# Pooled attention before two gated layers: the attention's order of work regrouped into six cycles of three key chunks

## The chip, the cores and the metric

The kernel runs on one core of a Trainium2 chip. The metric is the device time of one execution in microseconds. The kernel before was timed twice, 773.44 and 771.93 us, median 772.68 us. A further execution was profiled; its own time was 777.65 us and its span, from the first to the last instruction, 775.9 us.

## What is computed

Inputs are q, k and v of shape (2, 8, 1152, 64): two batches of eight heads. Attention pools q by two (576 query rows against 1152 keys), then two gated layers follow. Cut to what matters:

```python
q_pool = q.reshape(B, H, S // 2, 2, D).mean(axis=3)
scores = scale * np.matmul(q_pool, k.transpose(0, 1, 3, 2))
scores = scores - np.max(scores, axis=-1, keepdims=True)
attn = np.exp(scores); attn = attn / (np.sum(attn, axis=-1, keepdims=True) + 1e-09)
x = np.matmul(attn, v)           # -> (B * 576, 512)
xn = x / rms(x) * rms_g          # 1152 tokens, d_model 512, d_ff 1536
x = (silu(xn @ w_gate) * (xn @ w_val)) @ w_out
out = (sigmoid(x @ w_gate2) * (x @ w_val2)) @ w_out2
```

All is float32. Products that need the precision are made of three float32r products of split halves (high x high, high x low, low x high); turns and the products with v are plain float32. Weights arrive as 64-bit words and are turned into float32 and split on the core.

## The kernel before, in words

**Pairs.** The 16 heads are handled as 8 pairs; the two heads of a pair use the two 64-row lanes of TensorE at once (`LANES`). The 576 query rows of a head are chunks of 128, numbered 1 to 4, and 64 rows that are left; those of both heads together are chunk 0.

**Scores.** `s_unit` (L435 on) makes the scores of one query chunk against 384 keys: six products (L454) into two of the three `s` banks, for chunk 0 three products (L451) into one. For each bank `top` (L459, VectorE) writes the negated scores into an `e` tile and keeps the running minimum; from the second 384 keys on it starts from the minimum before, read as a pointer operand. After the third, `expo` (L463, ScalarE) takes the exponential of the 1152 columns in place, with row sums. A pair has 15 units, 27 tops, 9 exponentials; there are 10 `e` tiles.

**Turns and products with v.** `t_unit` (L480 on) turns 128 keys of the exponentials into a tile `t` of two PSUM banks (two such tiles exist), one bank a lane. `PARTS` gives two parts of a pair: chunks 1, 2 and 0 (ten turns a key chunk, L291, one copy of 640 columns), then 3 and 4 (eight turns, L498, two key chunks in one tile, one copy of 1024). The copy into `et` is ScalarE's (L510) or, where `E_DVE` says so, VectorE's (L508). `av_unit` (L526) multiplies v with the copies into the one `o` bank, in groups of two to five key chunks, right behind the copies (`AV_SLOTS`). `o_step` then turns the result back (L552), copies it (L563) and normalises it on GpSimd (L561).

**Order.** Every step is put by hand into an agenda: `at(g, rank, fn)`. Slots g run in order, ranks within a slot, then the order of registration; each engine executes its own instructions in the order in which the agenda emits them. A pair has 18 slots, one for each key chunk and part. The scores of the next pair lie in the slots of this one by a list:

```python
S_SLOTS = (-12, -9, -5, -8, -7, -6, -4, -3, -2, 0, 1, 2, 3, 4, 5)
AV_SLOTS = ({2: 3, 5: 6, 8: 9}, {3: 4, 8: 9})
E_DVE = ((2, 5, 8), (3, 7))
```

**Other work in the attention.** `prep_pair` turns k and q of the next pair (L291 into kT and qT, also in the two `t` tiles), ScalarE copies them (L350) and GpSimd splits them (L129, L130). `pool_q` (L325) sums q on GpSimd. `load_pair`, `load_v` and `w_load` issue on SP's queue. Five chunks of weights are converted during the attention (L197 to L240). `x_steps` does the rms norm: for the first batch during the last pairs, for the second at the end (L582 to L624, turns L603). From `END` on come the two layers (L683 to L822); their first four groups of products are interleaved with the last norm steps (`UP_SLOTS`).

Of the kernel before, what the change touches and what calls it, by code (L numbers as in the profile page):

```python
# [16 lines left out]
P = 128  # L17
# [5 lines left out]
S_SLOTS_FIRST = (-8, -7, -6, -5, -4, -3, -2, -1, 0, 1, 2, 3, 4, 5, 6)  # L23
S_SLOTS = (-12, -9, -5, -8, -7, -6, -4, -3, -2, 0, 1, 2, 3, 4, 5)
UNITS_FIRST = [(c, u) for u in range(3) for c in (3, 4)] + [(c, u) for c in (0, 1, 2) for u in range(3)]
UNITS = [(c, u) for c in range(5) for u in range(3)]
AV_SLOTS = ({2: 3, 5: 6, 8: 9}, {3: 4, 8: 9})
E_DVE = ((2, 5, 8), (3, 7))

PREP = ((1, 2, 3), (-5, -3, -1))  # L30
POOL_Q, LOAD, LOAD_V = -8, 0, 1
FIRST_K, FIRST_Q = (-7, -5), -4

W_SLOTS, W_SPLIT = (11, 12, 13, 14, 15), 8
W_WORDS, W_EARLY = 5, 4

X_SQUARES = ((-39, -37, -40), (-27, -30))
X_ROOTS = (-20, -17)
X_NORMS = ((-10, -15, -16), (-13, -11))
X_TURNS = ((-7, -12, -13), (-9, -8))  # L40
X_LAST = ((-3, -2, -2), (5, 6))

UP_SLOTS = (0, 2, 4, 7)
UP_GATES = (2, 4, 7, 9)
UP_SPLITS = (3, 5, 8, 10)
# [3 lines left out]
def tile_attention_moe_moe(ctx, tc, q, k, v, w_gate1, w_val1, w_out1, rms_g, w_gate2, w_val2, w_out2, out):  # L49
# [18 lines left out]
    NCA = 3  # L68
    PARTS = ((1, 2, 0), (3, 4))
# [29 lines left out]
    def two_banks(name):  # L99
        return ps.tile([P, 1024], F32, tag="t", bufs=2, name=name)  # L100
# [7 lines left out]
    osb = [ae.tile([P, 3 * P], F32, name="osb0"), ae.tile([P, 2 * P], F32, name="osb1")]  # L108
    nc.gpsimd.memset(osb[0][:, 5 * QH:6 * QH], 0.0)
# [172 lines left out]
    ready = {}  # L282
# [3 lines left out]
    def lanes(t, n, blocks):  # L286

        for x, (rows, cols) in enumerate(blocks):
            for j, r in enumerate(LANES):
                if rows[j] is not None:  # L290
                    nc.tensor.transpose(t[:, 512 - (1 - j) * 64 * n + x * 64:512 - (1 - j) * 64 * n + x * 64 + 64], rows[j][r, cols], ident[r, r])  # L291
        return t[:, 512 - 64 * n:512 + 64 * n]

    def turned(t):
        return t.rearrange("p (h c f) -> p h c f", h=2, f=QH)
# [4 lines left out]
    def load_pair(p):  # L300
        b, hp = divmod(p, NPAIR)
        kr = ap.tile([P, NK, P], F32, tag="kraw", bufs=1, name="kraw")
        qr = ap.tile([P, 2, NQC, 2 * D], F32, tag="qraw", bufs=1, name="qraw")
# [29 lines left out]
    def k_group(p, c0, c1, kr):  # L333
        t = lanes(two_banks("kT"), c1 - c0, [((kr[:, c], kr[:, c]), slice(0, P)) for c in range(c0, c1)])
        return t, kq[p][0][:, c0 * P:c1 * P], kq[p][1][:, c0 * P:c1 * P], 1.0

    def q_group(p, cs, qs):
        t = lanes(two_banks("qT"), len(cs), [((qs[:, c], qs[:, c]), slice(0, P)) for c in cs])
# [20 lines left out]
    def prep_pair(g0, p):  # L359
        alloc_pair(p)  # L360
        kr, qs = raw[p]
        slots = [g0 + x for x in PREP[p > 1]]
        at(slots[0], 3, lambda: prep_step(slots[0], k_group(p, 0, 5, kr)))
        at(slots[1], 3, lambda: prep_step(slots[1], q_group(p, (1, 2, 3, 4, 0), qs)))
        at(slots[1] + 1, 22, lambda: diagonal(p))
        at(slots[2], 3, lambda: prep_step(slots[2], k_group(p, 5, NK, kr)))

    def prep_first():


        def room():
            return ap.tile([P, NSU * SU], F32, tag="e", bufs=10, name="first")
# [4 lines left out]
        def load_q(j, c0, c1):  # L377
            qs = q[0, j].rearrange("(s two) d -> s (two d)", two=2)
            if c0 == 0:
                for r, x in ((slice(0, QH), SQ - QH), (slice(QH, P), 0)):  # L380
                    nc.sync.dma_start(qr[j][r, 0, :], qs[x:x + QH, :])
                c0 = 1
            nc.sync.dma_start(qr[j][:, c0:c1, :], qs[(c0 - 1) * P:(c1 - 1) * P, :].rearrange("(c p) e -> p c e", p=P))

        def load_k(j, c0, c1):
            nc.sync.dma_start(kr[:, c0:c1, j * D:(j + 1) * D], k[0, j].rearrange("(p c) d -> p c d", c=NK)[:, c0:c1])

        for j in range(2):
# [17 lines left out]
        def step(g, group, second):  # L406
# [6 lines left out]
            r = temp(t.shape[1])  # L413
# [18 lines left out]

        at(FIRST_Q, 1, rest)

    def s_unit(g, p, c, u):  # L435
# [20 lines left out]
        def top(j):  # L456

            m = emin[p, c, j]
            nc.vector.tensor_scalar(etile[p, c, j][:, kc], s[j], -1.0, m[:, u - 1:u] if u else None, op0=ALU.mult, op1=ALU.min, accum_out=m[:, u:u + 1])  # L459

        def expo(j):
            e = etile[p, c, j]
            nc.scalar.activation(e, e, AF.Exp, bias=emin[p, c, j][:, NSU - 1:NSU], scale=-1.0, accum_out=both_sums[p][:, j, c:c + 1])  # L463
# [5 lines left out]
        for j in heads:  # L469
            at(g, 17, lambda j=j: top(j))  # L470
        if u == NSU - 1:
            for j in heads:
                at(g + 1, 14, lambda j=j: expo(j))
            if c == 0:
                at(g + 2, 24, swap)
            ready.setdefault(p, []).append(c)
            if len(ready[p]) == NQC:
                at(g + 3, 25, lambda: nc.gpsimd.tensor_scalar(both_sums[p], both_sums[p], 1e-9, 1.0, op0=ALU.add, op1=ALU.mult))

    def t_unit(g, base, p, part, kc):  # L480

        ks = slice(kc * P, (kc + 1) * P)
        cs = PARTS[part]
        tiles = [(etile[p, c, 0], etile[p, c, 0]) for c in cs if c]
        tiles += [(etile[p, 0, 0], etile[p, 0, 0])] if 0 in cs else []
        tiles += [(etile[p, c, 1], etile[p, c, 1]) for c in cs if c]
        if part:

            odd = kc % 2
            n = 2 if odd or kc < NK - 1 else 1  # L490
            if not odd:
                tpair[p] = two_banks("eT"), []
            t, blocks = tpair[p]
            w = n * len(tiles) * 64
            for x, (a, b) in enumerate(tiles):
                for j, (y, r) in enumerate(((a, HP), (b, LP))):
                    o = 512 - (1 - j) * w + (odd * len(tiles) + x) * 64
                    nc.tensor.transpose(t[:, o:o + 64], y[r, ks], ident[r, r])  # L498
            if not odd and n == 2:
                return  # L500
            chunks = (kc - 1, kc) if odd else (kc,)
            t = t[:, 512 - w:512 + w]
        else:
            t = lanes(two_banks("eT"), len(tiles), [(x, ks) for x in tiles])
            chunks = (kc,)
        et = ae.tile([P, 1024], F32, tag="et", bufs=6, name="et")[:, 0:t.shape[1]]
        if kc in E_DVE[part]:
            at(g, 18, lambda: nc.vector.tensor_copy(woven(et), turned(t)))  # L508
        else:
            at(g, 12, lambda: nc.scalar.activation(woven(et), turned(t), AF.Copy))  # L510
        todo = ready.setdefault((p, part), [])
        n = et.shape[1] // len(chunks)
        todo += [(x, et[:, i * n:(i + 1) * n]) for i, x in enumerate(chunks)]
        if kc in AV_SLOTS[part]:
            now = list(todo)
            del todo[:]
            at(base + AV_SLOTS[part][kc], 4, lambda: av_unit(base + AV_SLOTS[part][kc], p, part, now))

    def av_unit(g, p, part, todo):
        if todo[0][0] == 0:  # L520
            acc_o[p, part] = bank("o", "o")
        o = acc_o[p, part]
        for kc, et in todo:
            n = et.shape[1] // 2
            for j, r in enumerate(LANES):
                nc.tensor.matmul(o[r, 0:n], vsb[p][:, j, kc], et[:, j * n:(j + 1) * n], start=(kc == 0), stop=(kc == NK - 1))  # L526
        if kc == NK - 1:
            at(g, 13, lambda: nc.scalar.activation(osb[part][:, 0:n], o[:, 0:n], AF.Copy))
# [339 lines left out]
```

## Time and profile before

| | |
|---|---|
| median of the two runs | 772.68 us |
| profiled execution, its own time | 777.65 us |
| its span | 775.9 us |
| TensorE busy (matmul / weight load) | 722.5 / 624.8 us |
| VectorE, ScalarE, GpSimd busy | 392.7, 382.9, 292.1 us |
| mean granted TensorE clock | 0.968 |
| attention's last product with v ends | 321.2 us |

In forty slices of the span TensorE is busy 7 to 9 tenths in the first 16, and 9 tenths or more in nearly all that follow; the granted clock is below full only in the first 17. A busy time in the profile overlaps with that of the next instruction, so what one instruction costs is read from the distance between two starts on the same engine, where neither waited. The clock's column is the share of full speed that was granted: 1.00 is the upper level, 2.4 GHz, and 0.50 the lower, 1.2 GHz.

### The profile page before, as it was taken

The page shows a single profiled execution, that of the slowest core. Times are in us where ns is not written, and L with a number is a line of the kernel's source. Part 1 is how long each engine was busy: PE and PEld are TensorE (multiplying, and loading weights), DVE is VectorE, ACT ScalarE, POOL GpSimd, SP SyncE. Part 2 cuts the span into 40 slices and gives each one's busy share as a digit, 9 for nine tenths or more (in the row PEclk, how much of TensorE's full clock was granted, in tenths as well). Part 3 has the DMA queues.
Part 4 walks back from the last instruction along what each step waited for, and adds up shares of the span by engine and source line. Part 5 has one row for each costly group of instructions (what it writes and reads, how often), then busy time and mean ns, then how long its engine had stood idle before and what let it go on. Part 6 is the DMA issues. An engine that isn't in the chain of part 4 may idle for free.

```text
span 775.9 us, 13594 instructions
## 1 busy us (share of the span) xinstructions
PE 722.5 (93%) x5420; PEld 624.8 (81%) x5420; DVE 392.7 (51%) x862; ACT 382.9 (49%) x684; POOL 292.1 (38%) x279
## 2 busy tenths in 40 slices
PE   7889797888888886999999999999999999999998
PEld 5666565555555563799999999999999999998886
DVE  5555565636464663468866675422345555454010
ACT  4665666656566654366544454432444454445000
POOL 3331514242424033046643455632434454347200
PEclk9999999979898997899999999999999999999999
DMA  8312314040401000033422232420312232223011
GB/s 193 103 42 56 86 39 104 21 106 19 105 18 59 2 2 1 10 99 117 128 82 82 82 109 82 129 90 28 109 55 81 83 108 62 76 82 109 0 55 68
DMA packets 66783, 55.92 MB, mean 72 GB/s; under 512 B 20896, under 2 KB 61856, under 8 KB 66720
## 3 DMA queue, kind: packets, MB, share of 16 engines
q1 hardware_dynamic: 66720, 55.06, 24.2%
q8 instruction: 42, 0.69, 0.4%
q14 instruction: 21, 0.17, 0.1%
HBM read 52.69 MB, written 2.36 MB: 71 GB/s over the span
## 4 chain that ended last, share of the span: by engine, by line
PE 82%; ACT 9%; issue 4%; DVE 4%; DMA 0%; POOL 0%; SPq 0%; ACTq 0%; DVEq 0%
PE acc L683 39%; PE o L526 10%; PE acc L793 10%; PE acc L822 9%; PE s L454 7%; ACT e L463 6%; ACT et L510 2%; PE eT L291 2%; PE eT L498 2%; PE s L451 1%; DVE e L459 1%; DVE et L508 1%; PE kT L291 1%; ACT kqt L350 1%; PE xT L603 0%
## 5 line engine op out<-in xcount | busy, mean ns | idle before, releaser
L683 PE MATMUL acc<-xh,w 128*128 128x384 f32 (+2 forms) x1184 | 295.3, 331 | 0.0
L683 PEld LDWEIGHTS acc<-xh,w 128*128 128x128 f32 x1184 | 211.8, 188 | 0.5 <-issue 0.4
L683 PE MATMUL acc<-xl,w 128*128 128x384 f32 (+2 forms) x592 | 195.6, 330 | 0.0
L240 POOL TENSOR_TENSOR w<-wr,w 128x512 fp32r<-128x512 f32 x68 | 99.9, 1469 | 166.9 <-ACT w L239 153.6
L459 DVE TENSOR_SCALAR_CACHE_REDUCE e<-s,m 128x384 f32<-128x384 f32 x144 | 83.8, 616 | 105.6 <-PE s L454 57.3
L683 PEld LDWEIGHTS acc<-xl,w 128*128 128x128 f32 x592 | 111.2, 188 | 0.0
L225 POOL TENSOR_TENSOR wr<-wsg,wr 128x512 uint32<-128x512 uint32 x72 | 93.6, 1300 | 45.5 <-DVE wsg L219 43.4
L454 PE MATMUL s<-kh,q 64*128 64x384 f32 x384 | 102.4, 409 | 8.5 <-DVE e L459 7.1
L526 PE MATMUL o<-et,vraw 128*64 128x256 f32 (+1 forms) x576 | 94.6, 474 | 0.7 <-DVE et L508 0.7
L463 ACT ACTIVATE e<-e,m 128x1152 f32<-128x1152 f32 x72 | 89.5, 1247 | 8.8 <-DVE e L459 8.8
L510 ACT ACTIVATE et<-eT 128x640 f32<-128x640 f32 (+2 forms) x72 | 54.7, 761 | 75.5 <-PE eT L498 43.6
L694 ACT ACTIVATE sg<-acc 128x384 f32<-128x384 f32 (+2 forms) x74 | 35.7, 482 | 102.4 <-PE acc L683 102.3
L454 PEld LDWEIGHTS s<-kh,q 64*128 64x128 f32 x384 | 56.0, 203 | 33.9 <-DVE e L459 21.4
L697 DVE TENSOR_TENSOR sg<-acc,sg 128x384 f32<-128x384 f32 (+2 forms) x74 | 40.4, 547 | 83.8 <-PE acc L683 78.6
L219 DVE SCALAR_TENSOR_TENSOR wsg<-wg,wsg 128x512 uint32<-128x512 uint32 x72 | 77.1, 1071 | 2.3
L793 PE MATMUL acc<-hh,w 128*128 128x384 f32 x288 | 73.2, 334 | 0.0
L197 ACT ACTIVATE wg<-wraw 128x512 f32<-128x512 f32 x72 | 48.3, 671 | 47.8 <-DVE wsg L219 42.5
L526 PEld LDWEIGHTS o<-et,vraw 128*64 128x64 f32 x576 | 42.9, 157 | 32.6 <-issue 10.7
L215 DVE TENSOR_SCALAR wsg<-wg 128x512 uint32<-128x512 uint32 x72 | 41.2, 572 | 35.0 <-POOL wr L225 34.9
L204 ACT ACTIVATE wr<-wraw 128x512 uint32<-128x512 uint32 x72 | 47.8, 665 | 9.5 <-POOL w L240 8.5
L793 PEld LDWEIGHTS acc<-hh,w 128*128 128x128 f32 x288 | 52.1, 188 | 0.0
L454 PE MATMUL s<-kl,q 64*128 64x384 f32 x192 | 50.9, 390 | 0.0
(104 smaller groups left out, 941.1 us busy)
## 6 DMA issues: line engine op xcount, KB each, us to landing
wraw<-in_moe_w_gate_dram SPq DMA_DIRECT2D x24, 512.0 KB, 3.6
wraw<-in_moe_w_val_dram SPq DMA_DIRECT2D x24, 512.0 KB, 3.6
wraw<-in_moe_w_out_dram SPq DMA_DIRECT2D x24, 512.0 KB, 3.5
vraw<-in_v_dram SPq DMA_DIRECT2D x16, 288.0 KB, 3.3
kraw<-in_k_dram SPq DMA_DIRECT2D x14, 288.0 KB, 4.9
qraw<-in_q_dram SPq DMA_DIRECT2D x14, 256.0 KB, 4.8
out_dram<-ob SPq DMA_DIRECT2D x9, 256.0 KB, 2.0
qraw<-in_q_dram SPq DMA_DIRECT2D x14, 64.0 KB, 4.5
```

The source lines that it names most:

```text
L197: nc.scalar.activation(g, wwords[n][:, :, 1].bitcast(F32), AF.Copy, scale=2.0 ** -112)
L219: nc.vector.scalar_tensor_tensor(x["s"], x["g"], 3, x["s"], op0=ALU.logical_shift_left, op1=ALU.bitwise_or)
L225: nc.gpsimd.tensor_tensor(x["r"], x["s"], x["r"], op=ALU.add)
L240: nc.gpsimd.tensor_tensor(t[:, 1], r, t[:, 0].bitcast(F32), op=ALU.subtract)
L454: nc.tensor.matmul(s[j], qt[r, x, QOF[c]:QOF[c] + P], ks[r, kc], start=(n == 0), stop=(n == 2))
L459: nc.vector.tensor_scalar(etile[p, c, j][:, kc], s[j], -1.0, m[:, u - 1:u] if u else None, op0=ALU.mult, op1=ALU.min, accum_out=m[:, u:u + 1])
L463: nc.scalar.activation(e, e, AF.Exp, bias=emin[p, c, j][:, NSU - 1:NSU], scale=-1.0, accum_out=both_sums[p][:, j, c:c + 1])
L510: at(g, 12, lambda: nc.scalar.activation(woven(et), turned(t), AF.Copy))
L526: nc.tensor.matmul(o[r, 0:n], vsb[p][:, j, kc], et[:, j * n:(j + 1) * n], start=(kc == 0), stop=(kc == NK - 1))
L683: nc.tensor.matmul(acc[:, 0:nt], wt[:, ws, dc * P:(dc + 1) * P], xs[:, dc], start=(dc == 0 and n == 0), stop=(dc == NDM - 1 and n == 2))
L793: nc.tensor.matmul(acc[t][:, 0:NTT], w[:, ws, (fc % 4) * P:(fc % 4 + 1) * P], hs[fc][:, cs], start=(fc == 0 and n == 0), stop=(fc == NFC - ...
L822: nc.tensor.matmul(acc[r][:, 0:DM], hs[fc][:, r * P:(r + 1) * P], w[:, ws, :], start=(fc == 0 and n == 0), stop=(fc == NFC - 1 and n == 2))
```

## The change

The agenda of the attention is made anew: a pair has six cycles of eight slots, a cycle turns three key chunks (cycles 0 to 2 for part 0, 3 to 5 for part 1). Chunk 0 moves to the second part, so `PARTS` is (1, 2) and (3, 4, 0). In a cycle the emitted order is: chunk 0's three units (cycle 1 only); turns of k, q or the result, if any; a first unit of scores; the turns of the first two key chunks into one `t` tile, half a bank each a lane; those of the third into the next `t` tile, with the three pieces of chunk 0 beside it in part 1; a second unit of scores; the products with v of the cycle before. Every key chunk is copied by itself: two by ScalarE, the third and chunk 0's pieces by VectorE. The running minimum becomes three separate maxima and a small reduction. There are 12 `e` tiles. q's load is issued behind `pool_q`, k's in cycle 1. The second batch's norm steps follow the last product directly. The core of the diff:

```diff
-S_SLOTS = (-12, -9, -5, -8, -7, -6, -4, -3, -2, 0, 1, 2, 3, 4, 5)
-AV_SLOTS = ({2: 3, 5: 6, 8: 9}, {3: 4, 8: 9})
-E_DVE = ((2, 5, 8), (3, 7))
-PREP = ((1, 2, 3), (-5, -3, -1))
+CYCLE, NCYC = 8, 6
+S_SUB, PREP_SUB, AV_SUB = (0, 4, 5), 0, 7
+S_UNITS = ((-5, 1, 1, 0), (-4, 0, 1, 1), (-4, 1, 1, 2), (-3, 0, 2, 0), (-3, 1, 2, 1), (-2, 0, 2, 2), (-2, 1, 3, 0),
+           (-1, 0, 3, 1), (-1, 1, 3, 2), (0, 0, 4, 0), (0, 1, 4, 1), (1, 0, 4, 2))
+C0_CYCLE = 1
+EXPS = {(1, 0): (-3, 1), (1, 1): (-3, 7), (2, 0): (-2, 7), (2, 1): (-1, 1), (3, 0): (0, 1), (3, 1): (0, 7),
+        (4, 0): (1, 7), (4, 1): (2, 1), (0, 0): (2, 7)}
+E_DVE = ((2,), (2,), (2,), (2, 3), (2, 3), (2, 3))
+PREP = ((0, 1, 2), (-3, -2, 0))
...
-    PARTS = ((1, 2, 0), (3, 4))
+    PARTS = ((1, 2), (3, 4, 0))
...
-            nc.vector.tensor_scalar(etile[p, c, j][:, kc], s[j], -1.0, m[:, u - 1:u] if u else None, op0=ALU.mult, op1=ALU.min, accum_out=m[:, u:u + 1])
+            nc.vector.tensor_scalar(etile[p, c, j][:, kc], s[j], 1.0, None, op0=ALU.mult, op1=ALU.max, accum_out=m[:, u:u + 1])
+            if u == NSU - 1:
+                nc.vector.tensor_reduce(m[:, NSU:NSU + 1], m[:, 0:NSU], op=ALU.max, axis=AX.X, negate=True)
...
-        for j in heads:
-            at(g, 17, lambda j=j: top(j))
+        for n, j in enumerate(heads):
+            at(g + (2 * n if g % CYCLE == S_SUB[0] else 0), 17 + n if c else 10, lambda j=j: top(j))
         if u == NSU - 1:
             for j in heads:
-                at(g + 1, 14, lambda j=j: expo(j))
+                at(max(g + 2, (p * NCYC + EXPS[c, j][0]) * CYCLE + EXPS[c, j][1]), 12, lambda j=j: expo(j))
...
+    def t_units(g, cyc, ns, p, part):
+        if ns[0] == 0:
+            ecyc[cyc] = [ae.tile([P, 5 * P], F32, tag="et", bufs=6, name="et") for _ in range(3)]
+        t = two_banks("eT")
+        copies = []
+        for n in ns:
+            kc = cyc % 3 * 3 + n
+            blocks = [(2 * (etile[p, c, j],), slice(kc * P, (kc + 1) * P)) for j in range(2) for c in PARTS[part] if c]
+            o = QH * part
+            copies.append((n, woven(ecyc[cyc][n][:, o:o + 4 * P]), lanes(t, 4 * (n == 1), blocks)))
+            av = (cyc + 1) * CYCLE + (AV_SUB if cyc + 1 < END // CYCLE else 0)
+            et = ecyc[cyc][n][:, 0:(5 if part else 4) * P]
+            at(av, 4, lambda kc=kc, et=et: av_unit(cyc + 1, p, part, kc, et))
+        if part and n == 2:
+            z = lanes(t, 4, [(2 * (etile[p, 0, 0],), slice(k * P, (k + 1) * P)) for k in range(kc - 2, kc + 1)])
+            e = ecyc[cyc]
+            copies.append((3, e, z))
+        for n, dst, src in copies:
+            def copy(n=n, dst=dst, src=src):
+                op = nc.vector.tensor_copy if n in E_DVE[cyc % NCYC] else lambda d, x: nc.scalar.activation(d, x, AF.Copy)
+                if n < 3:
+                    op(dst, turned(src))
+                else:
+                    for x, e in enumerate(dst):
+                        op(e.rearrange("p (h f) -> p h f", f=QH)[:, 0:10:9], src[:, :, x * QH:(x + 1) * QH])
+            at(g, 17 if n in E_DVE[cyc % NCYC] else 12, copy)
...
+            last = cyc == END // CYCLE
+            at((cyc + 1 - last) * CYCLE, 11, lambda: nc.scalar.activation(osb[part][:, 0:n], o[:, 0:n], AF.Copy))
+            g = (cyc + 2) * CYCLE + PREP_SUB if not last else END + 1
+            at(g, 1, lambda: o_step(g, p, part))
...
         if last:
+            for c in range(n):
+                at(g, 45, lambda c=c: square(c))
+                at(g, 47, lambda c=c: norm(c))
+                at(g + 1 + c, 3, lambda c=c: tr(g + 1 + c, c))
+            at(g, 46, root)
+            return
...
+        for x, n, c, u in S_UNITS_SECOND if p == 1 else S_UNITS:
+            g = (cyc0 + x) * CYCLE + S_SUB[n]
+            at(g, 2, lambda g=g, p=p, c=c, u=u: s_unit(g, p, c, u))
+        for u in range(NSU):
+            g = (cyc0 + C0_CYCLE) * CYCLE
+            at(g, 0, lambda g=g, p=p, u=u: s_unit(g, p, 0, u))
+        for cyc in range(cyc0, cyc0 + NCYC):
+            for ns, sub in (((0, 1), 1), ((2,), 3)):
+                g = cyc * CYCLE + sub
+                at(g, 3, lambda g=g, cyc=cyc, ns=ns, p=p: t_units(g, cyc, ns, p, int(cyc % NCYC >= 3)))
...
-UP_SLOTS = (0, 2, 4, 7)
+UP_SLOTS = (1, 3, 5, 7)
```

## Rows read from the trace of the kernel before

**Rows 1.** Windows: a pair each, then the layers; us, busy per engine, PEclk, DMA.
```profile
96.75:133.54 36.79, 31.35 (x355) 21.43 (x355) 20.76 (x62) 22.63 (x37) 12.84 (x16) 0.95 0.27 65
...
249.20:282.62 33.42, 28.88 (x328) 19.61 (x327) 19.89 (x61) 20.58 (x35) 2.90 (x6) 1.00 0.06 19
282.62:321.24 38.62, 30.53 (x314) 19.99 (x313) 19.03 (x46) 16.34 (x29) 12.91 (x15) 0.78 0.00 1
321.24:775.90 454.66, 450.86 (x2544) 437.64 (x2544) 218.62 (x344) 197.56 (x374) 188.72 (x137) 1.00 0.26 82
```

**Rows 2.** Waits of TensorE's matmuls, 100 to 282 us: total, times, longest.
```profile
PE kT L291 <- DVE et L508: 6.9, 4, 1.7
```

**Rows 3.** Timeline of TensorE in one pair: start, us, instruction, count.
```profile
137.36 1.84 PE L526 MATMUL o<-et,vraw 128*64 128x320 f32 x12
139.12 0.45 PE L454 MATMUL s<-kh,q 64*128 64x384 f32 x2
...
139.76 0.47 PE L291 MATMUL eT<-ident,e 64*128 64x64 f32 x10
...
148.21 0.44 PE L451 MATMUL s<-kh,qbd 128*128 128x384 f32 x1
...
148.93 0.44 PE L454 MATMUL s<-kh,q 64*128 64x384 f32 x2
...
149.55 0.41 PE L498 MATMUL eT<-ident,e 64*128 64x64 f32 x8
149.79 0.36 PE L552 MATMUL oT<-ident,osb 64*128 64x64 f32 x6
```

**Rows 4.** Timeline of VectorE in the same pair.
```profile
136.73 0.82 DVE L508 COPY et<-eT 128x640 f32<-128x640 f32 x1
137.47 0.55 DVE L459 TENSOR_SCALAR_CACHE_REDUCE e<-s 128x384 f32<-128x384 f32 x1
...
137.94 0.55 DVE L459 TENSOR_SCALAR_CACHE_REDUCE e<-s 128x384 f32<-128x384 f32 x1
...
150.82 0.21 DVE L536 RECIPROCAL rc<-sums 128x10 f32<-128x10 f32 x1
...
153.56 1.22 DVE L508 COPY et<-eT 128x1024 f32<-128x1024 f32 x1
```

**Rows 5.** Timeline of ScalarE in the same pair.
```profile
138.12 1.25 ACT L463 ACTIVATE e<-e,m 128x1152 f32<-128x1152 f32 x1
...
139.36 1.24 ACT L463 ACTIVATE e<-e,m 128x1152 f32<-128x1152 f32 x1
...
164.56 0.60 ACT L510 ACTIVATE et<-eT 128x512 f32<-128x512 f32 x1 [0.62 <-PE eT L498]
165.05 1.25 ACT L463 ACTIVATE e<-e,m 128x1152 f32<-128x1152 f32 x1
```

**Rows 6.** The chain of waits: start, us, the same five key chunks' products in two pairs.
```profile
131.24 2.31 PE o L526 x20
...
168.05 4.46 PE o L526 x20
```

**Rows 7.** Window behind a wait of TensorE; columns as in rows 1.
```profile
156.00:158.00 2.00, 2.00 (x13) 0.86 (x9) 0.00 (x0) 0.32 (x1) 1.51 (x2) 0.59 0.00 0
```

**Rows 8.** Timeline of the first 25 us, VectorE.
```profile
7.50 0.56 DVE L459 TENSOR_SCALAR_CACHE_REDUCE e<-s 128x384 f32<-128x384 f32 x1
...
12.58 0.62 DVE L459 TENSOR_SCALAR_CACHE_REDUCE e<-s,m 128x384 f32<-128x384 f32 x1 [0.57 <-PE s L454]
...
14.31 0.62 DVE L459 TENSOR_SCALAR_CACHE_REDUCE e<-s,m 128x384 f32<-128x384 f32 x1 [0.57 <-PE s L454]
```

**Rows 9.** Timeline of the first 25 us, TensorE.
```profile
13.26 0.69 PE L454 MATMUL s<-kh,q 64*128 64x384 f32 x1
...
20.09 0.37 PE L498 MATMUL eT<-ident,e 64*128 64x64 f32 x2 [0.76 <-ACT e L463]
```

**Rows 10.** Timeline of TensorE near the attention's end.
```profile
310.92 0.69 PE L498 MATMUL eT<-ident,e 64*128 64x64 f32 x8 [1.98 <-DVE et L508]
```

More of the change, by code (lines that the diff above doesn't have):

```diff
@@ L99, in two_banks @@
     def two_banks(name):
-        return ps.tile([P, 1024], F32, tag="t", bufs=2, name=name)
+        return ps.tile([P, 2, 512], F32, tag="t", bufs=2, name=name)
     ident = const.tile([P, P], F32, name="ident")
@@ L290, in lanes, with width, load_q @@
                 if rows[j] is not None:
-                    nc.tensor.transpose(t[:, 512 - (1 - j) * 64 * n + x * 64:512 - (1 - j) * 64 * n + x * 64 + 64], rows[j][r, cols], ident[r, r])
-        return t[:, 512 - 64 * n:512 + 64 * n]
+                    nc.tensor.transpose(t[:, j, (x0 + x) * 64:(x0 + x + 1) * 64], rows[j][r, cols], ident[r, r])
+        return t[:, :, x0 * 64:(x0 + len(blocks)) * 64]
     def turned(t):
-        return t.rearrange("p (h c f) -> p h c f", h=2, f=QH)
+        return t.rearrange("p h (c f) -> p h c f", f=QH)
     def woven(x):
         return x.rearrange("p (c h f) -> p h c f", h=2, f=QH)
-    def load_pair(p):
+    def width(t):
+        return 2 * t.shape[2]
+    def load_q(p):
         b, hp = divmod(p, NPAIR)
-        kr = ap.tile([P, NK, P], F32, tag="kraw", bufs=1, name="kraw")
-        qr = ap.tile([P, 2, NQC, 2 * D], F32, tag="qraw", bufs=1, name="qraw")
+        qr = raw["q", p] = ap.tile([P, 2, NQC, 2 * D], F32, tag="qraw", bufs=1, name="qraw")
         qs = q[b, 2 * hp:2 * hp + 2].rearrange("j (s two) d -> j s (two d)", two=2)
@@ L333, in k_group @@
     def k_group(p, c0, c1, kr):
[L334 removed]
+        t = lanes(two_banks("kT"), 0, [((kr[:, c], kr[:, c]), slice(0, P)) for c in range(c0, c1)])
         return t, kq[p][0][:, c0 * P:c1 * P], kq[p][1][:, c0 * P:c1 * P], 1.0
     def q_group(p, cs, qs):
[L338 removed]
+        t = lanes(two_banks("qT"), 0, [((qs[:, c], qs[:, c]), slice(0, P)) for c in cs])
         q0 = QOF[cs[0]]
@@ L412, in step @@
                 return
-            r = temp(t.shape[1])
+            r = temp(width(t))
             at(g, 13, lambda: nc.scalar.activation(woven(r), turned(t), AF.Copy, scale=sc))
@@ L474, in s_unit @@
             if c == 0:
[L475 to L517, printed above, removed]
@@ L521, in av_unit @@
+    def av_unit(cyc, p, part, kc, et):
+        if kc == 0:
             acc_o[p, part] = bank("o", "o")
         o = acc_o[p, part]
[L523 to L526, printed above, removed]
+        n = et.shape[1] // 2
+        for j, r in enumerate(LANES):
+            nc.tensor.matmul(o[r, 0:n], vsb[p][:, j, kc], et[:, j * n:(j + 1) * n], start=(kc == 0), stop=(kc == NK - 1))
@@ L535, in o_step @@
             rcp[p] = ae.tile([P, NQC, 2], F32, tag="rc", bufs=2, name="rc")
-            at(g, 18, lambda: nc.vector.reciprocal(rcp[p].rearrange("p c j -> p j c"), both_sums[p]))
+            rj = rcp[p].rearrange("p c j -> p j c")
+            at(g, 18, lambda: nc.vector.reciprocal(rj[:, :, 0:NQC - 1], both_sums[p][:, :, 1:NQC]))
+            at(g, 18, lambda: nc.vector.reciprocal(rj[:, :, NQC - 1:NQC], both_sums[p][:, :, 0:1]))
         if b not in xall:
             if b == B - 1:
-                xa = ae.tile([P, NCA, DM], F32, tag="xa", bufs=1, name="xa")
-                xb = ae.tile([P, NQC - NCA, DM], F32, tag="xb", bufs=1, name="xb")
+                xa, xb = [ae.tile([P, n, DM], F32, tag=f"xa{n}", bufs=1, name="xa") for n in (NCA, NQC - NCA)]
             else:
@@ L577, in x_steps @@
             alloc_x(0, 1)
+        ids = PARTS[part]
+        n = c1 - c0
         def square(c):
             sq = temp(DM)
-            if last and c0 + c != NCA:
+            if last and c % 2 == 0:
                 nc.vector.scalar_tensor_tensor(sq, xp[:, c], 1.0, xp[:, c], op0=ALU.mult, op1=ALU.mult, accum_out=ss[:, c:c + 1])
@@ L637, in x_steps @@
-        for c in range(n):
-            at(sq[c], 45 if last else 15, lambda c=c: square(c))
-        at(rt, 46 if last else 31, root)
-        for c in range(n):
-            at(nm[c], 47 if last else 22, lambda c=c: norm(c))
-            at(tt[c], 3, lambda c=c: tr(tt[c], c))
-    NJ = 2 * NK
-    END = NP * NJ
+            for c in range(n):
+                at(g, 45, lambda c=c: square(c))
+                at(g, 47, lambda c=c: norm(c))
+                at(g + 1 + c, 3, lambda c=c: tr(g + 1 + c, c))
@@ L647, in tile_attention_moe_moe @@
+            at(g, 46, root)
+            return
+        for c in range(n):
+            at((END // CYCLE + X_SQUARES[part][c]) * CYCLE + PREP_SUB, 15, lambda c=c: square(c))
+            at((END // CYCLE + X_NORMS[part][c]) * CYCLE + PREP_SUB, 22, lambda c=c: norm(c))
+            gt = (END // CYCLE + X_TURNS[part][c]) * CYCLE + PREP_SUB
+            at(gt, 4, lambda c=c, gt=gt: tr(gt, c))
+        at((END // CYCLE + X_ROOTS[part]) * CYCLE + PREP_SUB, 15, root)
+    END = NP * NCYC * CYCLE
     prep_first()
@@ L648, in tile_attention_moe_moe @@
     for p in range(NP):
-        g0 = p * NJ
-        for (c, u), sl in zip(*((UNITS, S_SLOTS), (UNITS_FIRST, S_SLOTS_FIRST))[p == 0]):
-            at(g0 + sl, 5 if c == 0 else 2, lambda g=g0 + sl, p=p, c=c, u=u: s_unit(g, p, c, u))
-        for n, part in enumerate((0, 1) if p else (1, 0)):
-            base = g0 + n * NK
-            for kc in range(NK):
-                at(base + kc, 3, lambda g=base + kc, base=base, p=p, part=part, kc=kc: t_unit(g, base, p, part, kc))
-        if p + 1 < NP:
-            first = min(PREP[p > 0])
-            if p:
-                at(g0 + POOL_Q, 50, lambda p=p: pool_q(p + 1))
-            else:
-                at(-2, 50, lambda: pool_q(1))
-            at(g0 + first, 0, lambda p=p, g0=g0: prep_pair(g0, p + 1))
-            at(g0 + LOAD_V, 51, lambda p=p: load_v(p + 1))
+        cyc0 = p * NCYC
```

164 lines of the change are left out of this document (78 added, 86 removed).

## The prediction

> **What bounds the kernel now.** I read the windows pair by pair first. The two layers take 454.7 us of the span with TensorE at work in 450.9 of them; the attention takes the first 321.2 us, and a pair 33.4 to 38.6 us [rows 1]. TensorE's busy figure there (28.9 of 33.4) is no measure of its work, since waiting products count as busy. So I took the distances between starts where nothing waited [rows 3, 6]. A unit of scores is 139.76 - 139.12 = 0.64 us; one of chunk 0 is 148.93 - 148.21 = 0.72; eight turns are 0.24, so one is 0.03; three key chunks' products with v are 139.12 - 137.36 = 1.76 at 320 columns, and at 256 columns five take 2.31, so three take 1.39.
>
> TensorE's work in a pair is then 12 x 0.64 + 3 x 0.72 = 9.9 for scores, 162 x 0.03 = 4.9 for turns, 3 x 1.76 + 3 x 1.39 = 9.4 for the products with v, and 38 turns of k, q and results = 1.1: **25.3 us** at the upper clock level, against (321.2 - 20.1) / 8 = 37.6 measured from the first full set of turns [rows 9]. Twelve microseconds a pair are waits and clock. TensorE waits for copies that must empty one of two `t` tiles [rows 2], and in bursts of scores it goes at VectorE's pace. After such a wait the granted clock falls to 0.59 in a window [rows 7], and the same products take 4.46 instead of 2.31 us [rows 6]. The pair without that loss stood at clock 1.00 and still took 33.4 [rows 1].
>
> **The change, part by part.** *TensorE* keeps its work: 15 units, 162 turns, the same columns of products with v (chunk 0's only change sides). By cycle it is 4.0, 5.6, 3.6, 3.9, 4.3 and 4.1 us, sum 25.5; what the change moves is what stands beside what. Two units a cycle are parted by 24 turns (0.7 us) on one side and by products with v (1.4 to 1.8 us) on the other, and these products use copies a cycle old.
>
> *VectorE.* The unchained top has a pitch of 137.94 - 137.47 = 0.47 [rows 4]; 27 make 12.7 us. Nine new reductions of three columns have no row; from below they are nothing, from above the 0.21 of the reciprocal of ten columns [rows 4]. I take 0.2, nearest in shape, so 1.8. Copies: (1.22 - 0.82) / 384 columns is 1.04 ns a column, and the 640-column copy has a pitch of 137.47 - 136.73 = 0.74 [rows 4], so 512 columns are 0.61 and 128 are 0.21: 6 x 0.61 + 9 x 0.21 = 5.5. Two reciprocals 0.4, two weight steps by the 0.61 of a like copy 1.2. Sum 21.6 a pair.
>
> *ScalarE.* Nine exponentials at 139.36 - 138.12 = 1.24 are 11.2; twelve copies at 165.05 - 164.56 = 0.49 are 5.9 [rows 5]; k and q (640, 640 and 512 columns) by the same rate 1.7, results 1.2, weights 1.0. Sum 21.0. Splitting 14 copies into 27 instructions thus stays beside TensorE's 25.3; if TensorE's cover were gone it would be the next bound.
>
> *Waits inside a cycle.* The second unit needs the first top of the first unit: 0.47 us plus hand-over, under 0.74 of turns. The next first unit needs the second unit's first top, under 1.4 of products. The first unit's second top and the third chunk's copy stand ahead of the second unit's tops: 0.47 + 0.61, in part 1 0.63 more; VectorE's cycle is at most 4.4 (cycle 1, seven tops) against 5.6 of TensorE, so this is covered. The third chunk's turns need the `t` tile that held k, q or a result in the same cycle, so ScalarE's copy of it. Ahead of that copy stands the exponential at the end of the cycle before. ScalarE's cycles 0, 2 and 3, with two exponentials, come to 3.9 to 4.1 us, as long as TensorE's; walking cycles 2 to 4 with these durations leaves TensorE waiting 0.2 us once.
>
> *Queues.* On SP, k's load goes out in cycle 1, behind v's, three cycles ahead of its turns, and q's behind `pool_q`, five cycles ahead of the next sum; neither has another load ahead of it that waits longer. GpSimd's splits follow the copies and have a cycle. I cost these at nothing; their cover is that lead, and a late k would make TensorE wait as in [rows 2], 1.7 at the longest.
>
> **The sum.** A pair lies between 25.3 (no wait) and 33.4 (today's pair at full clock). I take 28.5, nearer the floor: the waits of the 33.4 are bursts of scores and copies just made, and both are taken apart; 0.5 us a cycle is left for hand-overs.
>
> Start: the first top comes at 7.5 us, and units follow at 14.31 - 12.58 = 1.73 [rows 8], products there at 0.69 instead of 0.45, so at the lower level [rows 9, 3]. Nine units stand ahead of cycle 0, so it begins at 7.5 + 8 x 1.73 = 21.3, and 1.2 for k's later groups: 22.5. First pair: 25.3, less 1.8 (cycle 0 has no products with v), 4 more for about 8 us at the lower level, 1.5 waits: 29. Six pairs: 171. Last pair: no scores of a next one (9 x 0.64), nor its turns (0.8): 18.7; 1.5 for ScalarE's two exponentials in a thin cycle; TensorE waits in cycle 47 for part 0's norm (copy, GpSimd, VectorE, GpSimd, VectorE) ahead of its turns. Its nearest row is a wait of 1.98 [rows 10], between 2 and 5, I take 3.5; as much for the clock after it, and 1.3 of hand-overs: 28.5. First batch's norm, five chunks whose turns put a second user on the `t` tiles: 1 each, 5. Last product with v: 22.5 + 29 + 171 + 28.5 + 5 = **256**, against 321.2.
>
> Behind it three chunks are normed instead of two, and TensorE waits for the first ahead of its second group of products: by [rows 10] 2, bounds 0 to 5. So 256 + 2 + 454.7 = 712.7 of span, and with the 1.75 us that lie around it 714.4, against the profiled 777.65. That execution stands 4.97 above the median of the runs, so the forecast is **710 us**. With a pair of 26 to 31 and 4 us for the start and tail it is 689 to 731.
>
> **Rivals.** *The waits stay, only the clock is won.* ScalarE's exponentials stand in front of the copies in the same queue, and a late one holds both `t` tiles. A pair is then 33.4, as it is today at clock 1.00: 7 x 4.9 = 34 more, **744 us**. For it speaks that ScalarE fills three cycles; against it that nothing needs these copies before the next cycle.
>
> *The order doesn't part what it says.* VectorE's chunk 0 pieces go into tiles that ScalarE also writes, and stand ahead of the second unit's tops. If VectorE waits there for ScalarE, the length of one exponential each cycle, 6 x 1.24 = 7.4 a pair, a pair is 35.9 and the time 710 + 52 = **762**. Against: pieces exist in three cycles of six, and the columns are disjoint.
>
> *Slower: the clock stays at its lower level.* Today it falls after waits [rows 7] and rises in dense products. If turns spread over every cycle keep it down, a pair at the lower level is 25.3 x 4.46 / 2.31 = 48.9 us. It decides from (37.6 - 28.5) / (48.9 - 28.5) = 0.45 of the time on; at 0.6 a pair is 40.7 and the time **795 us**. Against: products other than turns are 19.3 us of a pair, 58% of the 33.4 us pair that was granted 1.00 throughout [rows 1], and would be 68% of 28.5. The Trainium skill ("TensorE: Matmul & The Clock Gate", Part 4: PE-mode transpose) says that turns do not count as TensorE being busy in the way that raises its clock. By that rule this rival would be met wherever turns fill the cycle; no trace here shows turns alone for long.
>
> **Numbers.** Chances: the forecast 0.62, waits stay 0.20, order fails 0.11, slower clock 0.07. About 2% is what a measurement of this kernel tells from no change, so faster ends at 757 and slower begins at 788: faster 0.62 + 0.20 = 0.82, same 0.11, slower 0.07. The range goes from 689 up over the second case to 748, and leaves out the last two.
>
> **What would show it.** Right: the last product with v near 256 us; pairs of 26 to 31; clock 1.00 in all middle windows; VectorE's waits for scores short; TensorE's waits at the `t` tiles under 1 us; the layers' 455 us unchanged. Wrong: TensorE waiting for ScalarE in every cycle (744); VectorE waiting for ScalarE ahead of chunk 0's pieces (762); windows at 0.50 between pairs (795); a start of cycle 0 past 25 us, or a stretch behind the last product longer by more than 5, would each move the sum by itself.

## The result and the profile after

The changed kernel takes 708.64 us (708.51 and 708.78), the kernel before 772.68; the ratio is 0.917, with a 95% interval of 0.913 to 0.921. The profiled execution has a span of 707.0 us, 68.9 less than before. The forecast was 710.

The windows of the kernel after: four pairs, each from cycle 1 of one pair to cycle 1 of the next, the last 29 us of the attention, then the rest; columns as in rows 1:

```profile
57.16:83.49 26.33, 26.27 (x355) 19.16 (x355) 21.32 (x82) 21.71 (x42) 11.94 (x15) 1.00 0.33 92
83.49:109.73 26.24, 26.15 (x355) 19.05 (x354) 21.27 (x82) 21.97 (x42) 13.23 (x16) 1.00 0.33 91
109.73:135.97 26.24, 26.14 (x355) 19.05 (x354) 21.27 (x82) 21.98 (x42) 13.21 (x16) 1.00 0.34 92
135.97:162.34 26.37, 26.26 (x354) 18.94 (x353) 21.62 (x83) 23.20 (x46) 13.62 (x17) 1.00 0.34 92
...
218.00:247.30 29.30, 24.71 (x291) 16.33 (x291) 14.79 (x49) 15.79 (x32) 2.72 (x6) 0.94 0.07 20
247.30:707.00 459.70, 452.99 (x2550) 439.69 (x2550) 220.35 (x348) 197.89 (x375) 189.15 (x137) 0.99 0.25 80
```

The longest pair of the kernel before, which rows 1 leave out:

```profile
133.54:172.51 38.97, 33.62 (x356) 22.48 (x355) 20.75 (x62) 22.75 (x37) 12.83 (x16) 0.88 0.26 67
```

A middle pair takes 26.24 us, where it took 33.4 to 39.0 before, at a granted clock of 1.00. VectorE (21.3) and ScalarE (22.0) have about as much to do as before (20.8 and 22.8). The sum of TensorE's own steps was 25.3, so 0.9 us of a pair is left for all waits and hand-overs. The attention's last product with v ends at 247.3 instead of 321.2, and the stretch behind it is 5.0 us longer.

The waits of TensorE's matmuls in the kernel after, from 30 to 260 us (total, times, longest), to set against rows 2:

```profile
PE xT L610 <- DVE xa L599: 6.1, 2, 3.6
PE eT L295 <- DVE xl L629: 3.7, 5, 0.9
PE s L467 <- DVE e L472: 2.6, 3, 1.1
PE qT L295 <- POOL qsum L333: 1.4, 1, 1.4
```

Five more rows follow, each one wait of at most 0.5 us; one of them is for a copy of a key chunk, 0.3 us, late in the attention. In the four middle pairs (57.16 to 162.34) the list is empty. The two large waits are in the second batch's norm, the next five in the first batch's. One cycle on TensorE, the counterpart of rows 3:

```profile
92.49 0.53 PE L295 MATMUL qT<-ident,qsum 64*128 64x64 f32 x10
92.83 0.42 PE L467 MATMUL s<-kh,q 64*128 64x384 f32 x2
...
93.43 1.11 PE L295 MATMUL eT<-ident,e 64*128 64x64 f32 x30
94.35 0.43 PE L467 MATMUL s<-kh,q 64*128 64x384 f32 x2
...
95.06 1.52 PE L528 MATMUL o<-et,vraw 128*64 128x256 f32 x12
96.50 0.53 PE L295 MATMUL kT<-ident,kraw 64*128 64x64 f32 x10
```

No row has a wait behind it. The units are 93.43 - 92.83 = 0.60 and 95.06 - 94.35 = 0.71 us, priced at 0.64. From the first turn of q to the first of k the cycle (cycle 3) is 4.01 us; the forecast's list had 3.9. On VectorE in the same stretch, the counterpart of rows 4:

```profile
91.73 0.08 DVE L472 DVE_READ_ACCUMULATOR e<-s 128x1 f32 x1
91.85 0.16 DVE L474 TENSOR_REDUCE m<-m 128x1 f32<-128x3 f32 x1
91.92 0.55 DVE L472 TENSOR_SCALAR_CACHE_REDUCE e<-s 128x384 f32<-128x384 f32 x1
...
94.68 0.69 DVE L516 COPY et<-eT 128x512 f32<-128x512 f32 x1
95.28 0.68 DVE L519 COPY et<-eT 128x128 f32<-128x128 f32 x3
95.88 0.55 DVE L472 TENSOR_SCALAR_CACHE_REDUCE e<-s 128x384 f32<-128x384 f32 x1
```

The reduction that had no row puts the next top off by 91.92 - 91.73 = 0.19 us; a copy of 512 columns is 0.60, three pieces of chunk 0 together 0.60.

### The profile page after: what moved, and what is told of

Same layout as the page of the kernel before. It is cut to its first block, busy times and chain, and to the rows that moved or that the text cites. A ratio compares the mean times of both kernels' runs of the same rounds, so it can differ in the third digit from the quotient of the medians.

```text
span 707.0 us, 13681 instructions
## 1 busy us (share of the span) xinstructions
PE 681.2 (96%) x5420; PEld 603.9 (85%) x5420; DVE 399.7 (57%) x1020; ACT 379.7 (54%) x708; POOL 294.1 (42%) x280
## 4 chain that ended last, share of the span: by engine, by line
PE 64%; DVE 0%; issue 0%
PE acc L683 42%; PE acc L793 11%; PE acc L822 10%; PE xT L610 0%; DVE xa L599 0%; DVE ob L832 0%
## 5 line engine op out<-in xcount | busy, mean ns | idle before, releaser
L472 DVE TENSOR_SCALAR_CACHE_REDUCE e<-s 128x384 f32<-128x384 f32 x216 | 114.3, 552 | 41.1 <-PE s L467 29.9
L467 PE MATMUL s<-kh,q 64*128 64x384 f32 x384 | 87.0, 400 | 6.0 <-DVE e L472 5.1
L528 PE MATMUL o<-et,vraw 128*64 128x320 f32 (+1 forms) x576 | 81.1, 418 | 0.0
L528 PEld LDWEIGHTS o<-et,vraw 128*64 128x64 f32 x576 | 37.5, 138 | 30.7 <-issue 10.1
L514 ACT ACTIVATE et<-eT 128x512 f32<-128x512 f32 x96 | 52.0, 598 | 21.1 <-PE eT L295 20.5
L467 PEld LDWEIGHTS s<-kh,q 64*128 64x128 f32 x384 | 50.8, 202 | 14.5 <-DVE e L472 11.9
L295 PE MATMUL eT<-ident,e 64*128 64x64 f32 x1296 | 54.3, 226 | 5.3 <-DVE xl L629 3.7
L295 PEld LDWEIGHTS eT<-ident,e 64*128 64x128 f32 x1296 | 51.4, 141 | 9.2 <-DVE xl L629 4.4
```

The costliest lines, as they stand in the source:

```text
L295: nc.tensor.transpose(t[:, j, (x0 + x) * 64:(x0 + x + 1) * 64], rows[j][r, cols], ident[r, r])
L467: nc.tensor.matmul(s[j], qt[r, x, QOF[c]:QOF[c] + P], ks[r, kc], start=(n == 0), stop=(n == 2))
L472: nc.vector.tensor_scalar(etile[p, c, j][:, kc], s[j], 1.0, None, op0=ALU.mult, op1=ALU.max, accum_out=m[:, u:u + 1])
L514: op = nc.vector.tensor_copy if n in E_DVE[cyc % NCYC] else lambda d, x: nc.scalar.activation(d, x, AF.Copy)
```

## Experiments

Each kernel differs from the kernel after by the lines shown (`...` marks what is left out), e7 from the kernel before. The kernel before was timed again with each series of runs (medians 774.2, 773.6 and 775.5 us), the kernel after was not, so a difference of up to 3 us from it is no more than the series differ by. Theory: TensorE's own work bounds a pair because nothing it needs was made just before. Rivals: the parting of the scores alone, the lag alone, the clock alone, or VectorE.

**e1, the products in the cycle of their copies.**

```diff
-            av = (cyc + 1) * CYCLE + (AV_SUB if cyc + 1 < END // CYCLE else 0)
+            av = cyc * CYCLE + AV_SUB
```

> One part undone: the products with v come at the end of the same cycle as their copies, not of the next. Theory (the gain is that TensorE no longer waits for what was just made, and a pair stands at its own 25.3 us of work): the products now wait for ScalarE's two copies, which in three cycles of six have an exponential of 1.24 us ahead of them, so about 1 us a cycle, a pair of 31 to 33 us instead of 26.2, about 745 us. Rival A (parting the scores is the whole gain, the lag is idle): 708, same pairs. Rival B (the clock is the whole gain): 708 unless the windows fall below 1.00.

768.9 us: 60 more, and pairs of 33.8 to 37.8. The trace shows that the edit had done two things. TensorE's longest waits, 60 to 170 us:

```profile
PE o L528 <- ACT osb L531: 17.2, 7, 2.5
PE o L528 <- ACT wr L208: 3.7, 3, 1.3
PE o L528 <- DVE et L519: 2.6, 3, 0.9
```

The result's copy had stayed a cycle later, so the one `o` bank was not free for the next part. That is no cost of the copies, the clock fell as well (mean 0.982), and e1 says nothing clean of the lag.

**e1b, the same with the result's copy moved along.**

```diff
-            av = (cyc + 1) * CYCLE + (AV_SUB if cyc + 1 < END // CYCLE else 0)
+            av = cyc * CYCLE + AV_SUB
...
-            at(av, 4, lambda kc=kc, et=et: av_unit(cyc + 1, p, part, kc, et))
+            at(av, 4, lambda kc=kc, et=et: av_unit(cyc, p, part, kc, et))
...
-            last = cyc == END // CYCLE
-            at((cyc + 1 - last) * CYCLE, 11, ...
+            last = cyc == END // CYCLE - 1
+            at((cyc + 1) * CYCLE, 11, ...
```

> The products with v in the cycle of their copies, as in e1, but the result's copy and turns come a cycle earlier with them, so that the one bank of the result is free: e1 showed TensorE waiting there 17.2 us in 110 (7 waits), 5.3 us a pair, which the lag has nothing to do with. Theory: what is left of e1's 60 us is the wait for the copies themselves, 60 - 7 x 5.3 = 23: about 730 us. Rival (the copies hold TensorE in every cycle, the bank only stood in front of that wait): 745 to 768.

729.6 us (ratio to before 0.943, 0.931 to 0.955); pairs of 29.7. TensorE's waits in the same stretch are now for the copies alone:

```profile
PE o L528 <- DVE et L519: 9.9, 11, 1.1
PE o L528 <- ACT et L514: 2.0, 6, 0.5
```

So the lag is worth 3.4 us a pair, 21 us. VectorE's pieces of chunk 0 are what the products wait for, not, as e1's expectation had it, ScalarE's copies behind an exponential.

**e2, both units of scores together, behind the turns.**

```diff
-S_SUB, PREP_SUB, AV_SUB = (0, 4, 5), 0, 7
+S_SUB, PREP_SUB, AV_SUB = (4, 5, 6), 0, 7
...
-            at(g + (2 * n if g % CYCLE == S_SUB[0] else 0), 17 + n if c else 10, lambda j=j: top(j))
+            at(g, 17 + n if c else 10, lambda j=j: top(j))
```

> One part undone: both units of scores of a cycle stand one behind the other, after the turns, not parted by them. Theory: the second unit needs a bank that VectorE's first top must free, 0.47 us and hand-over on either side less what is left of the first unit, so TensorE waits 0.5 to 0.6 us a cycle, 3 to 4 us a pair, 7 pairs: about 732 us. Rival (the lag is the whole gain): 708 to 711.

770.8 us, 62 more. The expected wait is there, longer than thought, and a second beside it (timeline of TensorE in e2):

```profile
101.98 0.46 PE L295 MATMUL eT<-ident,e 64*128 64x64 f32 x8 [0.25 <-ACT kqt L359]
102.25 0.42 PE L467 MATMUL s<-kh,q 64*128 64x384 f32 x2
...
103.71 0.44 PE L467 MATMUL s<-kh,q 64*128 64x384 f32 x1 [0.52 <-DVE e L472]
```

From unit to unit it is 1.46 us. The unit that had stood between k's turns and the key chunks' was the cover of ScalarE's copy of k, and it was gone too. Part of the 62 us is the clock: its mean is 0.979 in this trace, against 0.994, which by the share of the span comes to at most 12 us.

**e2b, both units together, ahead of the turns.**

```diff
-S_SUB, PREP_SUB, AV_SUB = (0, 4, 5), 0, 7
+S_SUB, PREP_SUB, AV_SUB = (0, 0.5, 0.75), 0, 7
...
-        g0 = -4 * CYCLE - 5
+        g0 = -5 * CYCLE
...
-            at(g + (2 * n if g % CYCLE == S_SUB[0] else 0), 17 + n if c else 10, lambda j=j: top(j))
+            at(g, 17 + n if c else 10, lambda j=j: top(j))
```

> Both units of scores stand together as in e2, but ahead of the key chunks' turns, so that ScalarE's copy of k or q has the same or more cover than in the kernel after (e2 had also taken that cover: 0.25 to 0.36 us at the turns). Theory: the second unit's wait for VectorE's first top is what e2 cost, 1.46 us from unit to unit in its trace instead of 0.64, 0.8 x 6 x 7 = 34: about 742 us, at most 770. Rival (the cover of k's and q's copies cost most of e2's 62 us): 712 to 718.

741.8 us (0.959, 0.946 to 0.971); pairs of 30.8. Between 60 and 170 us only one wait of TensorE's matmuls is listed:

```profile
PE s L467 <- DVE e L472: 10.5, 22, 0.6
```

Parting the units is worth 33 us: 4.6 us in each of the four middle pairs, 5.5 and 7.1 in the two with the first batch's norm, where the clock also fell. Where they stand matters as much: e2 to e2b is 29 us, of which the clock's mean (0.990 in e2b) leaves at most 9 to the clock.

**e3, the chained minimum back.**

```diff
-            nc.vector.tensor_scalar(etile[p, c, j][:, kc], s[j], 1.0, None, op0=ALU.mult, op1=ALU.max, accum_out=m[:, u:u + 1])
-            if u == NSU - 1:
-                nc.vector.tensor_reduce(m[:, NSU:NSU + 1], m[:, 0:NSU], op=ALU.max, axis=AX.X, negate=True)
+            nc.vector.tensor_scalar(etile[p, c, j][:, kc], s[j], -1.0, m[:, u - 1:u] if u else None, op0=ALU.mult, op1=ALU.min, accum_out=m[:, u:u + 1])
...
```

> One part undone: the chained minimum with its pointer operand in place of three maxima and a reduction. VectorE gets 18 x 0.07 us more and 9 x 0.1 to 0.2 less a pair, nearly even. Theory (TensorE is the bound, VectorE is covered): within 1 us of 708.6. Rival (VectorE's pace still sets the cycle): 2 to 8 us either way.

711.6 us, with a ratio of 0.920 (0.915 to 0.925) against 0.917 for the kernel after; the intervals overlap. The spans differ by 2.6 us, and pairs in its trace are 26.7. The surplus lies in the half pair that holds chunk 0's units (cycles 0 to 2: 14.0 instead of 13.5); the other half has 12.7 and 12.8. Cycle 1, where VectorE has seven tops, is 5.83 instead of 5.51, so VectorE's pace does enter there. By the medians "within 1 us" was wrong by two, but the times alone would not tell the two kernels apart.

**e5, all copies on ScalarE.**

```diff
-E_DVE = ((2,), (2,), (2,), (2, 3), (2, 3), (2, 3))
+E_DVE = ((),) * NCYC
```

> All copies of turned key chunks go to ScalarE, none to VectorE: 6 x 0.49 + 9 x 0.17 = 4.5 us more a pair on ScalarE (21.0 to 25.5), 5.5 less on VectorE. Theory (the bound is TensorE at 25.3 and ScalarE is the next): ScalarE now takes as long as TensorE, nothing in its queue may be late any more: pairs of 28 to 30 us, 722 to 735 us. Rival (only the busiest engine counts, waits don't): 708 to 712.

718.1 us (0.928, 0.916 to 0.940). A pair of e5 and, below, of e6, columns as above:

```profile
84.67:112.91 28.24, 26.45 (x355) 19.05 (x354) 16.51 (x67) 26.12 (x57) 13.23 (x16) 1.00 0.31 85
```

TensorE's largest wait there is for ScalarE's copies of k and q (6.2 us, 8 times, 60 to 170 us). The pair is as expected, the whole is not: it lies between the two ranges. Four pairs are 1.5 to 2.7 us longer, the two with the first batch's norm only 1.0 and 0.2.

**e6, one product a score instead of three.**

```diff
-        for n, (x, ks) in enumerate(((0, kh), (0, kl), (1, kh))):
+        for n, (x, ks) in enumerate(((0, kh),)):
...
```

> Leaves out two of the three products of every score (the low halves), so its output is not the reference's; TensorE has 12 x 0.34 + 3 x 0.35 = 5.1 us less a pair, 20.2. Theory (TensorE is the bound of a pair): the pair falls until ScalarE at 21 to 22 us bounds it, 23 to 24 us instead of 26.24: 7 x 2.7 = 19 less, and as the start's units are shorter some 3 more, 685 to 690 us. Rival (waits between the engines set the cycle): 703 to 708.

```profile
76.68:101.14 24.46, 22.27 (x301) 14.52 (x300) 21.32 (x82) 21.86 (x43) 13.20 (x16) 1.00 0.36 99
```

691.9 us (0.894, 0.883 to 0.906), 2 above the theory's range and 11 under the rival's. Taking 5.1 us of TensorE's work away shortens a pair by 1.8, so TensorE is the bound of a pair, but by little: at 24.5 TensorE waits again, for ScalarE's copies of k and q (5.1 us, 9 times, 60 to 170 us) and for GpSimd's sums of q (3.1 us, 5 times). TensorE's clock stays at 1.00 in that pair; it fell to 0.50 at 160.7 us, and again in the last pair.

**e7, the lag on the kernel before.**

```diff
-AV_SLOTS = ({2: 3, 5: 6, 8: 9}, {3: 4, 8: 9})
+AV_SLOTS = ({2: 5, 5: 8, 8: 11}, {3: 6, 8: 11})
```

> The kernel before with one part of the change alone: its products with v come two to three slots behind the copies instead of one. Theory (the parts depend on each other: any wait left in the order takes most of the gain, as e1b and e2b left 21 and 33 us of 64 when one part was undone): with the scores still in bursts at VectorE's pace and turns still waiting for the two tiles, a small gain, 755 to 768 us. Rival (the lag is worth its 21 us in any order): 750 to 753.

783.8 us against 775.5 of the kernel before in the same series: 8 us more, 1.011 (1.005 to 1.016), which at 2% counts as the same. Both expectations had a gain, and none came. TensorE's waits in e7 (60 to 170 us) and, in the second fence, in the kernel before over the same stretch:

```profile
PE s L454 <- DVE e L459: 3.3, 10, 1.1
PE eT L291 <- ACT kqt L563: 3.2, 3, 1.1
PE kT L291 <- DVE et L508: 2.6, 3, 0.9
...
PE eT L498 <- ACT kqt L563: 1.9, 3, 0.6
```

```profile
PE kT L291 <- DVE et L508: 5.2, 3, 1.7
PE s L454 <- DVE e L459: 2.5, 8, 0.6
...
PE eT L498 <- ACT kqt L350: 1.2, 3, 0.6
```

The wait of k's turns for VectorE's copy halves, but the key chunks' turns now meet the copy of the result in their `t` tile (L563, 5.1 us in the two rows), which had no row there. The edit had done two things, as in e1: the result's copy is issued in the slot of its last products and its turns one slot later, so both moved two slots along. What the lag costs or gives on the old order by itself is not shown. I read the rows so that the products had been cover for copies in the old order, and that moving them moved the wait; no run tests this.

**e4 and b1, the tail.**

```diff
-X_LAST = (-3, 1)
+X_LAST = ((1, 1), (5, 6, 7))
...
-                at(g + 1 + c, 3, lambda c=c: tr(g + 1 + c, c))
+                gt = END + X_LAST[part][c]
+                at(gt, 3, lambda c=c, gt=gt: tr(gt, c))
```

> An improvement from the trace: the second batch's turns of part 0 are moved out of cycle 47 to behind the last product with v, those of part 1 two groups of products later (END + 5 to END + 7). Theory (TensorE's waits of 3.61 and 2.48 us there, and the lower clock behind each, are on the path): 6 to 8 us less, about 701.5. Rival (the norm chain is on the path anyhow and the wait only moves to the fifth group of products): 705 to 708.6.

702.4 us (0.909, 0.905 to 0.913): 6.2 less than the kernel after. Of the kernel after, these are the rows that answer to rows 10, from TensorE's timeline:

```profile
240.45 0.66 PE L610 MATMUL xT<-ident,xa 128*128 128x128 f32 x4 [3.61 <-DVE xa L599]
...
242.82 4.39 PE L528 MATMUL o<-et,vraw 128*64 128x320 f32 x24
...
253.99 0.63 PE L610 MATMUL xT<-ident,xa 128*128 128x128 f32 x4 [2.48 <-DVE xa L599]
```

Both waits are gone in e4, which keeps one of 2.7 us (the last products for VectorE's copy of their own cycle). b1 has also the first batch's turns moved, from `+ PREP_SUB` to `+ 6`:

> e4's tail, and the first batch's norm turns moved from ahead of a cycle's key chunks to behind its second unit of scores, where they no longer take the tile that the third chunk's turns need. Theory: the five waits of TensorE for VectorE's low halves (3.7 us in all) go, 2 to 3 us under e4's 702.4: about 700. Rival (the wait moves to the next cycle's k or q turns): 702 to 704.

703.6 us (0.907, 0.904 to 0.911), as e4. The five waits for the low halves are gone, and 2.8 us of others at the norm's turns have come. Its span is 1.8 us shorter, and its pairs there are 30.5 and 28.0 us instead of 31.0 and 28.6; the timed runs don't tell it from e4.

**f1 and f2, filling the start.** Both are b1 with two more instructions ahead of each unit of the first pair before its first turns; f2 has `nc.tensor.transpose` in place of the product.

```diff
+FILL = 2
...
+        if g < 0:
+            for _ in range(FILL):
+                nc.tensor.matmul(spare[0][:, 0:P], ident, ident, start=True, stop=True)
...
```

> b1 with two float32 products of 128 columns with the identity, into a bank nobody reads, ahead of each of the first pair's units of scores before its first turns, where TensorE waits for VectorE at the lower clock level (the units there have a pace of 1.7 us, their products 0.69 instead of 0.44). Theory (TensorE's own work raises its clock): the level is up some units earlier, the pace falls to about 1.4, 2 to 4 us under b1. Rival (VectorE's tops set the pace, or the level doesn't rise): 0 to 1 us over b1.

> b1 with two turns of 128 columns in the place of f1's two products. By the Trainium skill (TensorE: Matmul & The Clock Gate, Part 4: PE-mode transpose) turns do not count as work that raises the clock. If so: as b1, or up to 1 us over it, and the level rises no earlier than there. If turns count: between f1 and b1.

f1 has 703.5 us (698.6 to 705.8 over four runs; 0.906, 0.901 to 0.911), f2 700.2 (699.3 to 701.6; 0.903, 0.900 to 0.906). The time of f1 scatters too much for a verdict; f2 has the shortest time of the kernels that leave nothing out, but its interval and b1's overlap. The traces are clear on the clock. The fillings in f2, from TensorE's timeline:

```profile
13.27 0.69 PE L466 MATMUL warm<-ident 128*128 128x128 f32 x2
15.15 0.53 PE L466 MATMUL warm<-ident 128*128 128x128 f32 x2
16.59 0.44 PE L466 MATMUL warm<-ident 128*128 128x128 f32 x2
```

They become shorter from about 15 us on, in f1 from 8.4. In b1 the first product of a unit is still at 0.69 us at 23.4, and the shorter durations come only at 26, behind the first full set of turns. The first turns of key chunks start at 24.2 in b1, 22.8 in f2, 22.0 in f1: f2 lies between the two, as expected if turns count. The spans are 701.3, 697.6 and 696.8. Not all of this is the start: by cycle 1 of the last pair f2 is 2.3 us ahead of b1, and the other 1.4 come in the last pair, where b1's clock is at 0.50 from 241.2 to 244.6 us and f2's stays at 1.00. Why it does is not shown.

## Why the prediction was right, step by step

**TensorE's floor.** The sum of 25.3 us a pair from distances between starts was right: 26.24 with no wait listed in the middle pairs, and e6 shows by taking work away that it binds, with 1.8 us to the next bound.

**The size of a pair.** 28.5 was 2.2 too much. I had left 0.5 us a cycle for hand-overs; 0.9 a pair was needed. Over the six pairs that were priced so it is 13.5 us, the largest error of the sum.

**The start.** q's turns that open cycle 0 begin at 22.53; the forecast had 22.5. The first pair, with its lower clock until about 26, came 1 to 2 us longer than the 29.

**The first batch's norm.** 5 us forecast; the two pairs with it (cycle 1 to cycle 1, from 162.2 to 193.2 and on to 221.8) are 31.0 and 28.6 us, 7 over two middle pairs.

**The last pair and the tail.** The wait for part 0's norm was priced 3.5 and is 3.61; the last pair as a whole came about 1 us longer. Behind the last product 2 us were forecast, bounds 0 to 5, and 5.0 came, just past the sign that was named: the wait of 2.48, and the lower clock after it (products start 0.48 us apart at 255.2 us, 0.26 before, and the granted clock is 0.70 in 256 to 260 us). So the errors are -13.5 for the pairs, +2 for the first batch's norm, +1.5 and +1 for the first and last pair, +3 for the tail: 6 us together, a span of 707.0 where 712.7 was forecast.

**The last step, which was luck.** From 714.4 the forecast went down by 4.97 to 710, because the profiled execution of the kernel before stood so far above the median. I can name no term of the sum that held this excess, since pairs and layers were priced at clock 1.00, and the kernel after's own profiled execution, 708.78, is at its median, 708.64. The step cancelled most of the 6 us. Without it the forecast is 714 and 0.8% long, still inside its range; that is how close the sum was.

**A cost put at nothing.** The queues and GpSimd were priced at nothing. In the middle pairs that held; in the pair with the first batch's norm TensorE waited once for GpSimd's sum of q, 1.38 us at 172.9.

**The clock.** The mean rose from 0.968 to 0.994. At the lower level half the time is lost at most, so 0.032 x 775.9 less 0.006 x 707.0 = 20.6 us is the most that the clock itself gave back; at least 48 of the 69 are not the clock's.

**The rivals.** Waits stay (744): no; TensorE's list of waits is empty in the middle pairs. The order fails (762): not seen, VectorE never waited for ScalarE there; but its pieces of chunk 0 are what e1b's products wait for, so the place was a weak one. Slower clock (795): no; with turns in every cycle it was granted 1.00 in all the middle pairs, and in the pair shown of e6, with two thirds of the products of scores left out, too.

**What stays open.** Undone singly in the new order, the lag and the parting give back 21 and 33 us of the 64; each is then worth something without the other. No run undid both, so whether they add up is not shown. Nor were the other parts undone: the 12 `e` tiles, the copies by single key chunks, chunk 0 in the second part, the moved loads. On the old order the lag, with the result's step moved along, gained nothing, and no run had both parts on it.

## To carry to other kernels

Work out the floor of each engine from distances between starts in stretches without waits; where the bound engine's floor is far under the stage, order it so that whatever it reads was made a cycle ago, and put its other work between two users of the same bank. Then look for the one place that still reads what was just made: one such wait in most cycles gave back a third (e1b) or a half (e2b) of the gain here, and moving one step can take cover from another. After that, price the tail: it held 6 us that one moved step returned.

## What the runs showed of the hardware

At the start the granted clock's column reads 1.00 although the products are longer than later (in b1 the first product of a unit 0.69 us, in the middle pairs of the kernel after 0.42), so before the first recorded change the durations are what tells the level.

With turns as the only filling the level rose at about 15 us, eleven before it does without filling; with products at about 8. The Trainium skill ("TensorE: Matmul & The Clock Gate", Part 4: PE-mode transpose) has it that the full clock does not engage for turns. Scores stood between the turns here, so turns alone were not tried; beside other work they did help, later than products. That the products helped sooner may lie in their kind or in their amount: before the level rose, f1's fillings took 1.15 us ahead of a unit (5.38 to 6.53) and f2's 0.65 (5.47 to 6.12).
